# Two changes in a fused attention and two-layer MLP kernel: bf16 products of layer two left out, and another order in its last tile

## The chip, the cores and the metric

The kernel runs on one core of a Trainium2 chip. The metric is the device time of one execution, in microseconds (us). The time before is the median of three runs.

## The reference, cut to what matters

The kernel computes a two-part attention and two MLP layers behind it. The attention (4 batches, 8 heads, 576 positions, head dimension 64) adds a pooled part and a local part; its result, 2304 tokens of 512 features, goes through two layers of the same form:

```python
def mlp(x, w_in, w_out):          # x 2304 x 512, w_in 512 x 2048, w_out 2048 x 512
    h = np.maximum(x @ w_in, 0.0)
    return h * h @ w_out

x = attention(q, k, v)            # (2304, 512)
x = mlp(x, moe_w_in, moe_w_out)   # layer one
return mlp(x, moe2_w_in, moe2_w_out)   # layer two
```

Only the end of layer two and eight small products inside layer two are touched by the change.

## The kernel before, in words

**Tiles and steps.** The 2304 tokens are cut into nine tiles of 256. The list `seq` holds 18 pairs of layer and tile: entries 0 to 8 are layer one, 9 to 17 layer two, so n = 17 is the last tile of layer two. The 2048 hidden features are cut into eight pieces p of 256. A *step* is one pair (n, p): the products that make 256 hidden features of a tile (`mm_h`), ReLU and square on ScalarE (`act_h`), and the products with the second weight that add this piece to the tile's output.

**Number format.** All large products are made in three: each operand is split into a high and a low part, and high x high, high x low and low x high are summed. In `mm_h` that makes 12 products for each of the two halves of a piece, 24 per step, all from line 886.

**Layer two's output.** In layer two the second matrix product is made with seven block products in place of eight, which the code calls M1 to M7. `mm_y2` (line 944) issues them at line 952: with `first` true M5, M6, M7 and M3 (12 products of TensorE), with `first` false M1, M2 and M4 (9 products); 21 in all per step. They accumulate over the eight pieces in PSUM. `seven(n, m)` says where: M1 to M4 lie in one PSUM tile of two halves (M1 and M2 in the first, M3 and M4 in the second), `at0` for odd n and `y` for even n; M5 to M7 lie in `at1`.

**The end of a tile.** `leave` (line 1041) builds the four quarters c11, c12, c21 and c22 of the tile's output in the SBUF buffer `yst`: copies of M1 on ScalarE (line 1053, for the last tile also 1056), then seven sums on VectorE (line 1074) and the store. The last tile has a path of its own: copies of M1 to c11 and c21, the sum c11 + M2 first, then the wait for all products (`("y", n, NP - 1)`), the other six sums, a 256 KB store of the upper half of the rows behind the fourth sum (line 1069) and one of the lower half at the end (line 1077).

**What sets the order.** The program order of every engine's queue comes from the class `Order`, a planner that runs when the kernel is built. Each piece of work is a generator that yields the engine it wants and an estimated duration, or a condition (`o.at(key)`) to wait for; the planner emits what it thinks can start first. Events such as `ev["yA",]` or `ev["gl", i]` are planner events: they order the emission and are no waits on the chip. Waits on the chip are put in by the framework from what each instruction reads and writes. In `products` the generator `y` issues the second products of a step; for the last step (`i == last`) it issues M1, M2, M4 first, sets `yA`, waits for the event `gl` (the low part of the last sums S), and then issues M5, M6, M7, M3.

**The bf16 products.** `KICK` (line 49) names the steps (n, 3) for n = 10 to 17. In these, ahead of the first product of `mm_h`, line 879 issues one product of the 128 x 128 bf16 identity with itself into the first 128 columns of the PSUM tile that `mm_h` then overwrites. Its result is used by nothing. There are eight of them, one per tile from the second tile of layer two on.

Of the kernel before, what the change touches and what calls it, by code (L numbers as in the profile page):

```python
# [15 lines left out]
ALU = mybir.AluOpType  # L16
# [5 lines left out]
TN = 256  # L22
NT = B * S // TN
NP = DFF // 256
# [21 lines left out]
FT = 3  # L46
LAZY = dict(split_x=1.2)
FINE, HALF = 6, 1
KICK = {(n, 3) for n in range(10, 18)}
CL, GL, HL = 4, 4, 6  # L50
CP, CD, GP, UP = -0.848, 0.436, -1.416, -1.019
QP, VP, HP = -0.537, 0.649, -0.76
# [167 lines left out]
def attention_two_mlp_kernel(  # L220
# [11 lines left out]
    nc = tc.nc  # L232
# [6 lines left out]
    ident16 = sb.tile([128, 128], BF16, name="ident16")  # L239
# [120 lines left out]
    def seven(n, m):  # L360

        t = pair[2 - 2 * (n % 2) if m < 4 else 1]
        return t[:, m % 4 // 2, m % 2 * 256:m % 2 * 256 + 256]
# [5 lines left out]
    o = Order()  # L369
    ev = o.ev  # L370

    def dve(cols):
        return "DVE", 0.065 + cols / 957.0
# [23 lines left out]
    def dma(nbytes, run=4096):  # L397

        return "SP", nbytes / (16e3 * run) * {256: 22.5, 1024: 88.0, 2048: 142.0, 4096: 212.0}[run]
# [439 lines left out]
    seq = [(layer, t) for layer in (1, 2) for t in range(NT)]  # L839
# [32 lines left out]
    def mm_h(i, fi):  # L872
        n, p = steps[i]
        h, x = xH[n % NXL], xL[n % NXL]
        wH, wL = weight(p, 0, 0), weight(p, 0, 1)
        o = hb[i % 2][:, fi * 256:fi * 256 + 256]
        if (n, p) in KICK and fi == 0:

            nc.tensor.matmul(out=o[:, 0:128], lhsT=ident16, rhs=ident16, start=True, stop=True)
        fs = slice(fi * 128, fi * 128 + 128)  # L880
        mms = []
        for kk in range(4):
            mms += [(wH, h, kk), (wL, h, kk)]
        mms += [(wH, x, kk) for kk in range(4)]
        for i, (w, x, kk) in enumerate(mms):
            nc.tensor.matmul(  # L886
                out=o, lhsT=wt[p, 0][:, 1084:1340][:, fs] if w is wL and kk == 0 and p in ODD else w[:, kk, fs],
                rhs=x[:, kk], start=(i == 0), stop=(i == len(mms) - 1)
            )
# [51 lines left out]
                nc.vector.tensor_tensor(out=late2["SL"], in0=late2["S"], in1=late2["SH"].bitcast(F32), op=ALU.subtract)  # L941
            ev["gl", i] = tt

    def mm_y2(i, first):

        n, p = steps[i]
        some = ((5, 0, "T1"), (6, 1, "T2"), (7, 2, "T3"), (3, 3, "B22")) if first else ((1, 0, "B11"), (2, 2, "B21"), (4, 3, "T4"))
        for m, a, w in some:
            cs = slice(128 * a, 128 * a + 128)
            hi, lo = (late2["SH"][:, cs], late2["SL"][:, cs]) if first else (g_of(i, 0)[:, cs], g_of(i, 1)[:, cs])  # L950
            for x, (lhsT, low) in enumerate(((hi, 0), (hi, 1), (lo, 0))):
                nc.tensor.matmul(  # L952
                    out=seven(n, m - 1), lhsT=lhsT, rhs=quarter(p, w, low),
                    start=p == 0 and x == 0 and m not in (2, 3, 6),
                    stop=p == NP - 1 and x == 2 and m in (2, 4, 6, 7), skip_group_check=True,
                )
# [24 lines left out]
    def products():  # L981
        def y(i):
            n, p = steps[i]
            yield o.at("gh", i)
            if p == 0 and n > 1 and n < NT:
                yield o.at("left", n - 1 if n != 2 else 0)
            if seq[n][0] == 2:
                if p == 0 and n > NT:
                    yield o.at("left", n - 2)
                yield o.at("T", p)  # L990
                yield o.at("gl" if i != last else "gla", i)
                for first in (0 < p and i != last, p == 0 or i == last):
                    if p == 0 and first and n > NT:
                        yield o.at("left3", n - 1)
                    if i == last and first:
                        ev["yA",] = t
                        yield o.at("gl", i)
                    t = yield "PE", 1.37 if first else 1.03
                    mm_y2(i, first)
                    if first:  # L1000
                        ev["yS", i] = t
                ev["y", n, p] = t
                return
            yield "PE", 1.825
            mm_y(i, False)
            yield o.at("gl", i)
            ev["y", n, p] = yield "PE", 0.912
            mm_y(i, True)

        for i, (n, p) in enumerate(steps):  # L1010
            o.now.prio = n + p / NP + PO
            if p == 0 and i and n < NT:
                yield from y(i - 1)
            if i == last:
                yield o.at("gl", i - 2)
                yield "PE", 1.37
                mm_h(i, 0)
                ev["h", n, p] = yield "PE", 1.37
                mm_h(i, 1)
                yield from y(i - 2)  # L1020
                yield from y(i - 1)
                break
            if p == 0:
                yield o.at("split", n)
            if i == 0:
                o.fill = None
                yield from f_at.give_up([2])
            if (n, p) == (1, 0):
                yield from f_at.give_up([1])
            yield o.at("w", seq[n][0], p)  # L1030
            if i > 1:
                yield o.at("gl", i - 2)
            yield "PE", 1.37
            mm_h(i, 0)
            ev["h", n, p] = yield "PE", 1.37
            mm_h(i, 1)
            if (p or n >= NT) and i != last - 1:
                yield from y(i - 1)
        yield from y(last)

    def leave():
        for n, (layer, t) in enumerate(seq):
            yield o.at(*(("yA",) if n == len(seq) - 1 else ("y", n, NP - 1)))
            i = yield from f_ld.take()
            yst = ld[i].bitcast(F32)
            if layer == 1:
                for u in range(2):
                    tt = yield act(512)
                    nc.scalar.copy(yst[:, u * 512:u * 512 + 512], ybs(n)[u])
            else:  # L1050
                c11, c12, c21, c22 = (yst[:, 256 * m:256 * m + 256] for m in range(4))
                yield act(256)
                nc.scalar.copy(c11, seven(n, 0))
                if n == len(seq) - 1:
                    yield act(256)
                    nc.scalar.copy(c21, seven(n, 0))
                sums = [
                    (c21, c11, 6, ALU.add), (c12, c21, 5, ALU.add), (c21, c21, 7, ALU.add), (c22, c21, 5, ALU.add),
                    (c12, c12, 3, ALU.add), (c11, c11, 2, ALU.add), (c21, c21, 4, ALU.subtract),
                ]  # L1060
                if n == len(seq) - 1:
                    sums = [sums[k] for k in (5, 0, 1, 4, 2, 3, 6)]
                    sums[1] = (c21, c21, 6, ALU.add)
                for k, (dst, a, m, op) in enumerate(sums):
                    if n == len(seq) - 1 and k == 1:
                        yield o.at("y", n, NP - 1)
                    if n == len(seq) - 1 and k == 4:
                        yield dma(128 * 2048, 2048)
                        nc.sync.dma_start(out=out[t * TN:t * TN + 128], in_=yst[:, 0:512])
                        o.now.done, o.now.last = tt, "DVE"  # L1070
                    tt = yield dve(256)
                    if dst is c22:
                        ev["left3", n] = tt
                    nc.vector.tensor_tensor(out=dst, in0=a, in1=seven(n, m - 1), op=op)
                if n == len(seq) - 1:
                    yield dma(128 * 2048, 2048)
                    nc.sync.dma_start(out=out[t * TN + 128:(t + 1) * TN], in_=yst[:, 512:1024])
                    return
            ev["left", n] = tt
            if n == 1:  # L1080
                f_at.back(1, tt)
            tt = yield dma(128 * 4096)
            if layer == 1:
                nc.sync.dma_start(out=ys[t], in_=yst)
            else:
                nc.sync.dma_start(
                    out=out[t * TN:(t + 1) * TN].rearrange("(u p) e -> p u e", p=128),
                    in_=yst.rearrange("p (u e) -> p u e", u=2),
                )
            f_ld.put(i, tt)  # L1090
            ev["stored", n] = tt

    heads, groups, vees = [], [], []
    for b in range(B):
        t = b * S / TN - 2 + (b == 1) * H1
# [33 lines left out]
    with tc.manual_schedule():  # L1129
# [3 lines left out]
        for n, (c, off, some) in enumerate(((0, 0, (0,)), (0, 3, (1, 2)), (1, 3, (0, 1)), (1, 10, (2,)))):  # L1133
            m = xr[n % 2].rearrange("p k c -> p (k c)")[:, 64 * n:64 * n + 64]
            nc.gpsimd.memset(m, 0.0)
            first = off - 64 * c
            nc.gpsimd.affine_select(
                out=m, in_=m, pattern=[[1, 64]], base=3 - first, channel_multiplier=-1,
# [39 lines left out]
```

## Time and profile before

| | us |
|---|---|
| median of three runs | 907.33 (907.09 to 908.36) |
| the profiled execution, its own time | 912.61 |
| its span, first to last instruction | 910.8 |
| TensorE busy | 888.7 (98%) |
| VectorE busy | 488.4 (54%) |
| ScalarE busy | 520.6 (57%) |
| GpSimd busy | 61.9 (7%) |

In the profile PE is TensorE's matmul, PEld its weight load, DVE VectorE, ACT ScalarE, POOL GpSimd, SP the engine that issues the DMAs; a q behind a name means the engine's sequencer. Times count from the first instruction. Layer two begins at about 485 us. A matmul's row has its start and its length; since matmuls are pipelined, the length (0.28 us) is longer than the distance from one start to the next, so a rate is read from starts or from counts, not from lengths. In a row of the timeline several like instructions are merged: start, time that they cover, and their number behind the x.

### The profile page before, as it was taken

The page shows a single profiled execution, that of the slowest core. Times are in us where ns is not written, and L with a number is a line of the kernel's source. Part 1 is how long each engine was busy: PE and PEld are TensorE (multiplying, and loading weights), DVE is VectorE, ACT ScalarE, POOL GpSimd, SP SyncE. Part 2 cuts the span into 40 slices and gives each one's busy share as a digit, 9 for nine tenths or more (in the row PEclk, how much of TensorE's full clock was granted, in tenths as well). Part 3 has the DMA queues.
Part 4 walks back from the last instruction along what each step waited for, and adds up shares of the span by engine and source line. Part 5 has one row for each costly group of instructions (what it writes and reads, how often), then busy time and mean ns, then how long its engine had stood idle before and what let it go on. Part 6 is the DMA issues. An engine that isn't in the chain of part 4 may idle for free.

```text
span 910.8 us, 20739 instructions
## 1 busy us (share of the span) xinstructions
PE 888.7 (98%) x8701; PEld 857.3 (94%) x8701; DVE 488.4 (54%) x1035; ACT 520.6 (57%) x969; POOL 61.9 (7%) x70
## 2 busy tenths in 40 slices
PE   8888899999999999999999999999999999999997
PEld 5578899999999999999999999999999999999996
DVE  5695673475874535233323665546555464645454
ACT  3896884466467665644435674545554554545443
POOL 3310310020220100000001000000000000000000
PEclk9989899999999999999999999999999999999999
DMA  9999951353465675621214630101010000100000
GB/s 181 230 228 193 218 134 35 93 142 87 104 205 175 218 223 197 197 82 30 82 35 163 210 121 24 47 2 47 1 47 24 24 25 24 44 5 24 1 25 24
DMA packets 94013, 90.47 MB, mean 99 GB/s; under 512 B 62432, under 2 KB 70368, under 8 KB 93920
## 3 DMA queue, kind: packets, MB, share of 16 engines
q1 hardware_dynamic: 93920, 89.15, 36.2%
q8 instruction: 68, 1.11, 0.5%
q14 instruction: 25, 0.20, 0.1%
HBM read 70.25 MB, written 18.87 MB: 98 GB/s over the span
## 4 chain that ended last, share of the span: by engine, by line
PE 89%; DMA 6%; SPq 2%; DVE 1%; ACT 1%; issue 0%; ACTq 0%
PE h L886 42%; PE y L969 19%; PE at L952 14%; PE y L952 5%; DMA ld<-in_v_dram 3%; PE at L969 2%; DMA s<-in_moe_w_out_dram 2%; DMA s<-in_moe_w_in_dram 2%; PE at L455 1%; SPq L442 1%; PE at L646 1%; PE at L591 1%; PE at L481 1%; PE at L521 1%; PE at L628 1%; PE at L511 1%
## 5 line engine op out<-in xcount | busy, mean ns | idle before, releaser
L886 PE MATMUL h<-xH,w 128*128 128x256 f32 x2304 | 317.5, 280 | 2.1 <-ACT xH L395 2.1
L886 PEld LDWEIGHTS h<-xH,w 128*128 128x128 f32 x2304 | 287.4, 189 | 4.6 <-ACT xH L395 2.2
L969 PE MATMUL y<-g,w 128*128 128x256 f32 x1536 | 191.2, 279 | 0.0
L969 PEld LDWEIGHTS y<-g,w 128*128 128x128 f32 x1536 | 181.0, 188 | 2.7 <-issue 1.2
L886 PE MATMUL h<-xL,w 128*128 128x256 f32 x1152 | 180.4, 279 | 2.0 <-DVE xL L863 2.0
L886 PEld LDWEIGHTS h<-xL,w 128*128 128x128 f32 x1152 | 154.4, 189 | 2.5 <-DVE xL L863 2.5
L904 ACT ACTIVATE ld<-h 128x512 f32<-128x512 f32 x72 | 43.1, 598 | 133.1 <-PE h L886 133.1
L931 DVE TENSOR_TENSOR S<-ld 128x128 f32<-128x128 f32 x144 | 35.7, 289 | 153.2 <-ACT ld L906 153.2
L936 DVE TENSOR_TENSOR g<-h,g 128x512 fp32r<-128x512 f32 x72 | 49.6, 689 | 117.0 <-ACT g L908 116.6
L904 ACT ACTIVATE h<-h 128x512 f32<-128x512 f32 x72 | 42.0, 583 | 97.8 <-PE h L886 97.6
L914 ACT CAST SH<-S 128x512 fp32r<-128x512 f32 x72 | 44.8, 622 | 39.2 <-DVE S L931 29.8
L941 DVE TENSOR_TENSOR gSL<-S,SH 128x512 fp32r<-128x512 f32 x72 | 49.8, 692 | 10.8 <-ACT SH L914 2.2
L936 DVE TENSOR_TENSOR g<-ld,g 128x512 fp32r<-128x512 f32 x72 | 49.2, 684 | 0.1
L906 ACT ACTIVATE ld<-ld 128x512 f32<-128x512 f32 x72 | 45.5, 631 | 2.3
L908 ACT CAST g<-ld 128x512 fp32r<-128x512 f32 x72 | 44.8, 622 | 2.3
L952 PE MATMUL at<-w,SH 128*128 128x256 f32 x224 | 44.0, 278 | 0.0
L906 ACT ACTIVATE h<-h 128x512 f32<-128x512 f32 x72 | 42.2, 586 | 1.3
L908 ACT CAST g<-h 128x512 fp32r<-128x512 f32 x72 | 42.0, 584 | 1.4
L952 PE MATMUL at<-w,g 128*128 128x256 f32 x240 | 34.0, 277 | 0.0
L952 PEld LDWEIGHTS at<-w,SH 128*128 128x128 f32 x224 | 33.9, 188 | 0.0
L952 PE MATMUL at<-w,gSL 128*128 128x256 f32 x112 | 31.2, 279 | 0.1
L952 PEld LDWEIGHTS at<-w,g 128*128 128x128 f32 x240 | 30.4, 188 | 0.0
(251 smaller groups left out, 1276.7 us busy)
## 6 DMA issues: line engine op xcount, KB each, us to landing
s<-in_moe_w_in_dram SPq DMA_DIRECT2D x32, 256.0 KB
s<-in_moe_w_out_dram SPq DMA_DIRECT2D x16, 512.0 KB
ws<-ga SPq DMA_DIRECT2D x32, 256.0 KB
ld<-in_moe_w_in_dram SPq DMA_DIRECT2D x12, 512.0 KB
ld<-in_moe_w_out_dram SPq DMA_DIRECT2D x10, 512.0 KB
w<-ws SPq DMA_DIRECT2D x10, 512.0 KB
xr<-ys SPq DMA_DIRECT2D x9, 512.0 KB
vw<-in_v_dram SPq DMA_DIRECT2D x68, 64.0 KB
```

The costliest lines, as they stand in the source:

```text
L442: nc.sync.dma_start(out=raw[:, z].rearrange("p (h d) -> p h d", h=H), in_=(q, k)[z][b, :, 128 * c:128 * c + n].rearrange("h s d -> s h d"),)
L455: nc.tensor.transpose(pair[a][:, z, 128 * m:128 * m + n], raw[:, z, 128 * m:128 * m + 128], ident[0:n, 0:n])
L886: nc.tensor.matmul(out=o, lhsT=wt[p, 0][:, 1084:1340][:, fs] if w is wL and kk == 0 and p in ODD else w[:, kk, fs], rhs=x[:, kk], start=(i ...
L904: nc.scalar.activation(out=g, in_=h, func=AF.Relu)
L906: nc.scalar.activation(out=g, in_=g, func=AF.Square)
L908: nc.scalar.copy(g_of(i, 0), g)
L914: nc.scalar.copy(late2["SH"], late2["S"])
L931: nc.vector.tensor_tensor(out=dst, in0=a, in1=b, op=op)
L936: nc.vector.tensor_tensor(out=g_of(i, 1), in0=g, in1=g_of(i, 0).bitcast(F32), op=ALU.subtract)
L941: nc.vector.tensor_tensor(out=late2["SL"], in0=late2["S"], in1=late2["SH"].bitcast(F32), op=ALU.subtract)
L952: nc.tensor.matmul(out=seven(n, m - 1), lhsT=lhsT, rhs=quarter(p, w, low), start=p == 0 and x == 0 and m not in (2, 3, 6), stop=p == NP - ...
L969: nc.tensor.matmul(out=yb[e // 2][:, (e % 2) * 256:(e % 2) * 256 + 256], lhsT=w[:, fi, e * 128:e * 128 + 128], rhs=g[:, fi * 256:fi * 256 ...
```

## The change

Three edits:

1. `KICK` and the bf16 product of line 879 are left out.
2. In the last step `y` issues M1, M2, M4 as before, then M6, M7, M5 (`mm_y2` with `some`), sets `yB`, then waits for the planner's event `copied`, and then issues M3 alone. `copied` is set by `leave` behind the two copies of M1 and the sum c11 + M2, which so stand ahead of M3 in program order.
3. The last tile's copies go to c11 and c12 (not c21), the sums come in another order, and there are three stores in place of two: the upper 128 rows in full, then the left and the right half of the lower 128 rows.

```diff
-KICK = {(n, 3) for n in range(10, 18)}
...
-        if (n, p) in KICK and fi == 0:
-
-            nc.tensor.matmul(out=o[:, 0:128], lhsT=ident16, rhs=ident16, start=True, stop=True)
...
-    def mm_y2(i, first):
+    def mm_y2(i, first, some=None):
...
-        some = ((5, 0, "T1"), (6, 1, "T2"), (7, 2, "T3"), (3, 3, "B22")) if first else ((1, 0, "B11"), (2, 2, "B21"), (4, 3, "T4"))
-        for m, a, w in some:
+        all = ((5, 0, "T1"), (6, 1, "T2"), (7, 2, "T3"), (3, 3, "B22")) if first else ((1, 0, "B11"), (2, 2, "B21"), (4, 3, "T4"))
+        for m, a, w in [all[j] for j in some] if some else all:
...
                     if i == last and first:
+
                         ev["yA",] = t
                         yield o.at("gl", i)
+                        t = yield "PE", 1.03
+                        mm_y2(i, True, (1, 2, 0))
+                        ev["yB",] = t
+                        yield o.at("copied")
+                        t = yield "PE", 0.34
+                        mm_y2(i, True, (3,))
+                        break
...
                 if n == len(seq) - 1:
                     yield act(256)
-                    nc.scalar.copy(c21, seven(n, 0))
+                    nc.scalar.copy(c12, seven(n, 0))
+                    rows = out[t * TN:(t + 1) * TN].rearrange("(u p) e -> u p e", u=2)
+                    for dst, a, m, op, wait, to in (
+                        (c11, c11, 2, ALU.add, None, None), (c12, c12, 6, ALU.add, ("yB",), None),
+                        (c22, c12, 7, ALU.add, None, None), (c12, c12, 5, ALU.add, None, None),
+                        (c12, c12, 3, ALU.add, ("y", n, NP - 1), (rows[0], yst[:, 0:512])),
+                        (c21, c22, 4, ALU.subtract, None, (rows[1][:, 0:256], c21)),
+                        (c22, c22, 5, ALU.add, None, (rows[1][:, 256:512], c22)),
+                    ):
+                        if wait:
+                            yield o.at(*wait)
+                        tt = yield dve(256)
+                        nc.vector.tensor_tensor(out=dst, in0=a, in1=seven(n, m - 1), op=op)
+                        if m == 2:
+                            ev["copied",] = 0.0
+                        if to:
+                            yield dma(128 * 1024, 1024)
+                            nc.sync.dma_start(out=to[0], in_=to[1])
+                            o.now.done, o.now.last = tt, "DVE"
+                    return
...
-                if n == len(seq) - 1:
-                    sums = [sums[k] for k in (5, 0, 1, 4, 2, 3, 6)]
-                    sums[1] = (c21, c21, 6, ALU.add)
-                for k, (dst, a, m, op) in enumerate(sums):
-                    if n == len(seq) - 1 and k == 1:
-                        yield o.at("y", n, NP - 1)
-                    if n == len(seq) - 1 and k == 4:
-                        yield dma(128 * 2048, 2048)
-                        nc.sync.dma_start(out=out[t * TN:t * TN + 128], in_=yst[:, 0:512])
-                        o.now.done, o.now.last = tt, "DVE"
+                for dst, a, m, op in sums:
...
-                if n == len(seq) - 1:
-                    yield dma(128 * 2048, 2048)
-                    nc.sync.dma_start(out=out[t * TN + 128:(t + 1) * TN], in_=yst[:, 512:1024])
-                    return
```

## Rows read from the trace of the kernel before

**Rows 1.** The page: busy shares, and the chain's shares by engine.

```profile
PE 888.7 (98%) x8701; PEld 857.3 (94%) x8701; DVE 488.4 (54%) x1035; ACT 520.6 (57%) x969; POOL 61.9 (7%) x70
...
PE 89%; DMA 6%; SPq 2%; DVE 1%; ACT 1%; issue 0%; ACTq 0%
```

**Rows 2.** Windows: from:to, length, busy us (instructions) by engine, granted clock, DMA.

```profile
440.00:580.00 140.00, 140.00 (x1236) 140.00 (x1235) 68.25 (x141) 79.62 (x145) 5.17 (x7) 1.00 0.32 106
584.00:624.00 40.00, 40.00 (x342) 40.00 (x341) 20.44 (x53) 19.56 (x33) 0.00 (x0) 1.00 0.08 27
626.00:665.00 39.00, 39.00 (x346) 39.00 (x346) 20.72 (x53) 19.63 (x34) 0.00 (x0) 1.00 0.08 28
...
877.00:897.00 20.00, 20.00 (x179) 20.00 (x178) 8.81 (x23) 9.26 (x15) 0.00 (x0) 1.00 0.01 2
...
582.24:880.62 298.38, 298.38 (x2576) 298.10 (x2574) 160.85 (x406) 149.81 (x248) 0.00 (x0) 1.00 0.07 24
```

**Rows 3.** Line 879, the bf16 products: count, length, first and last start.

```profile
L879 PE MATMUL h<-ident x8: 230/230/230, 582.2 to 875.4; 128*128 128x128 bf16 x8
```

**Rows 4.** Timeline of TensorE: where steps of layer two begin.

```profile
582.24 0.23 PE L879 MATMUL h<-ident 128*128 128x128 bf16 x1
...
587.67 0.52 PE L886 MATMUL h<-xH,w 128*128 128x256 f32 x3
...
624.77 0.23 PE L879 MATMUL h<-ident 128*128 128x128 bf16 x1
...
630.02 1.07 PE L886 MATMUL h<-xH,w 128*128 128x256 f32 x8
...
665.78 0.23 PE L879 MATMUL h<-ident 128*128 128x128 bf16 x1
```

**Rows 5.** The chain that ended last, from the copies on: start, us, what.

```profile
904.83 0.76 DVE ld L1074 x2
...
905.61 0.43 DVE ld L1074
...
906.07 0.76 DVE ld L1074 x2
...
907.30 0.42 DVE ld L1074
```

**Rows 6.** Timeline of ScalarE and TensorE at the end.

```profile
904.15 0.37 ACT L1053 COPY ld<-at 128x256 f32<-128x256 f32 x1 [2.75 <-PE at L952]
904.42 0.38 ACT L1056 COPY ld<-at 128x256 f32<-128x256 f32 x1
...
902.42 0.28 PE L952 MATMUL at<-q_vw,g 128*128 128x256 f32 x1
902.53 0.40 PE L952 MATMUL at<-w,SH 128*128 128x256 f32 x2
...
903.59 0.40 PE L952 MATMUL at<-w,SH 128*128 128x256 f32 x2
903.83 0.28 PE L952 MATMUL at<-w,gSL 128*128 128x256 f32 x1
```

**Rows 7.** Timeline of TensorE: two restarts after a wait.

```profile
438.37 1.00 PEld L969 LDWEIGHTS y<-g,w 128*128 128x128 f32 x8 [0.19 <-ACT g L908]
...
899.13 0.19 PEld L952 LDWEIGHTS at<-w,gSL 128*128 128x128 f32 x1 [0.28 <-DVE gSL L941]
...
899.13 0.38 PE L952 MATMUL at<-w,gSL 128*128 128x256 f32 x1
```

**Rows 8.** SP's stores and its wait, and the DMA strip of 907 to 910.8.

```profile
907.75 0.34 SPq L1077 DMA_DIRECT2D out_dram<-ld  x1
...
SPq L1173 <- DMA out_dram<-ld: 1.6, 1, 1.6
...
DMA  0002989999920000289999992000000000000000
```

## The prediction

> **What bounds the kernel now.** I read the page's busy shares and its chain first: TensorE is busy for 98% of the span and holds 89% of the chain that ends last [rows 1]. So in layer two a time is a number of products times the distance between their starts. The windows show the clock granted in full (1.00, the 2.4 GHz level) in each of these stretches of layer two, and no other engine near its limit: VectorE and ScalarE are busy 20 of 39 to 40 us [rows 2]. But the products do not come at one rate: the stretch 440 to 580 holds 1236 in 140 us, 584 to 624 holds 342 in 40 us, 626 to 665 holds 346 in 39 us, and 877 to 897 has 179 in 20 [rows 2]. What lies between them and nowhere else is the bf16 product of line 879: there are eight, one in each tile, the first at 582.24 and the last at 875.37 [rows 3].
>
> The timeline of TensorE gives the size. A step of layer two is 24 products of line 886 and 21 of line 952, 45 in all. From 587.67, the step behind the first bf16 product, to the second at 624.77 there are 7 steps in 37.10 us: 5.300 each, 0.1178 us a product, the **wide** spacing. From 630.02 to the third at 665.78 there are 7 in 35.76 us: 5.109 each, 0.1135 us a product, the **narrow** one [rows 4]. Each bf16 product turns narrow into wide or wide into narrow, and what it set holds to the next one; this pair of tiles comes four times. The steps that begin with one take 5.43 us (582.24 to 587.67) and 5.25 us (624.77 to 630.02), so its own slot costs 0.13 to 0.14 us over the spacing that follows it [rows 4].
>
> The end is the second place where a wait counts. After the last product starts at 903.83, ScalarE's two copies, seven VectorE sums and a store follow one another: copy at 904.15, the first sum at 904.83, the last sum over at 907.72, and the store behind it [rows 5, 6].
>
> **The change part by part.** *The eight bf16 products out.* From the first one to the end of the last one's step the core spends 298.38 us (582.24 to 880.62) on 57 steps [rows 2, 4]. Without them nothing that the trace shows would turn the spacing: it is narrow when the first one comes, and it held through 140 us without one [rows 2]. Then the 57 steps take 57 x 5.109 = 291.2 us: **7.2 us less**, of which 4 x 0.13 + 4 x 0.14 = 1.1 us is the products' own slots and 32 x 0.191 = 6.1 us the steps with wide spacing. The whole is TensorE time on the chain, so no cover is needed or lost; what the other engines must do per step fits, since in the narrow stretch 626 to 665 they have half of the time free [rows 2]. The steps from 880.62 on are narrow already (179 in 20 us) and stay [rows 2]. Bounds: if wide spacing came without a cause for all 57 steps, 57 x 5.300 = 302.1, 3.7 us more than now; if none, 7.2 less. I take the latter, by the stretch ahead of the first one, 440 to 580.
>
> The Trainium skill's page "TensorE: Matmul & The Clock Gate", section "Back-to-back issue gap", gives one distance per shape, N/2.4 plus about 2.5 ns, so 109 ns for 256 columns. By it the kernel would have no second spacing to lose, and the whole edit would be worth the slots alone. The trace disagrees: one shape at one granted clock stands at 0.1135 and at 0.1178.
>
> *Copies and one sum ahead of M3.* Now the copy of M1 waits 2.75 us for TensorE, and starts at 904.15, behind the last product of M3 (903.83 and 0.28 long), though the first product behind M4 starts at 902.53 [rows 5, 6]. M1 to M4 of this tile share the PSUM tile at0; I read the wait as one on all products into that tile that stand ahead in the program. With M3 behind the copies they wait for M4's last product alone (902.42 + 0.28 = 902.70). The copies then stand at 902.73 and 903.00, and the first sum, which now follows the second copy's end by 0.03 [rows 6], at 903.41 instead of 904.83: 1.42 us earlier. ScalarE is free then: its wait of 2.75 began at 901.40.
>
> *M3 behind them.* If the tile's writers wait for its readers in the same way, M3's three products, which would be due at 903.59, wait for that sum (903.41 + 0.42) and start near 903.88 with one slower start (0.38 for the first product after a wait [rows 7]), and end near 904.5, 0.4 us later than now. Queued behind them on TensorE is nothing; only the fifth sum waits for them. M6, M7, M5 fill the gap: nine products from 902.53 on, the last one over by 903.76 (903.59 less 0.12, and 0.28 long).
>
> *The sums.* There are seven as before. Starts lie 0.34 apart where a sum doesn't need the one before it and 0.45 where it does (904.83 to 905.61 holds two, then 906.07) [rows 5]. In the new order: c11 + M2 at 903.41, c12 + M6 at 903.80, c22 at 904.25, c12 + M5 at 904.70, c12 + M3 at 905.16 (M3 was over at 904.5, so no wait), c21 at 905.50, c22 at 905.95, over at 906.37 against 907.72: 1.35 us earlier. So the later M3 is hidden by three sums; without that cover it would cost 0.4.
>
> *Three stores in place of two.* One issue on SP takes 0.34 us [rows 8]. The first is issued at 905.61, the second at 905.96, the third at 906.40, each ready when SP is. In the profile a 256 KB store begins to move 0.8 us behind its issue, moves for 0.75 us, and SP's wait for it is over 1.6 us behind the issue's end [rows 8]. The last one has 128 KB, half of the movement (-0.35 us by that rate), but it comes behind 384 KB which start at 906.4 and need 1.1 us: it moves from 907.5 to 907.9 and has landed 0.5 later, near 908.4 instead of 909.8. I take **1.4 us less** at the end. Bounds: 1.7 (sums and the half store in full) and 0.3 (the copies wait for M5's last product too, at 903.76; the sums start at 904.47, M3 waits for them, and only the half store remains). The nearest row is the copy's own wait, so I stay at 1.4.
>
> The Trainium skill's "PSUM — Partial Sum Buffer", section "PSUM bank collisions raise a hardware error", asks for guards by bank and quadrant only, and M3 lies in the other bank of that tile. By it the copies would need M2 alone, 0.36 us earlier, and the end would gain about 1.8. The trace disagrees: the copy of M1 waited 2.75 us, for M3.
>
> The sum is 7.2 + 1.4 = 8.6 us. The profiled execution took 912.61 us with a span of 910.8; the median of the three runs is 907.33, 5.28 lower. Nothing tells that the 5.28 lie in layer two, so I take 8.6 off the median: **898.7 us**.
>
> **The rivals.** *Wide spacing from the start (slower).* Which spacing holds is settled where TensorE restarts after a wait: the restart at 438.37 gave the narrow one [rows 2, 7], the one at 899.13 the wide one (902.53 to 903.59, nine products, 0.1178 each) [rows 6, 7]. If the timed runs enter layer two wide, before is 4 x (5.25 + 35.76 + 5.43) + 3 x 37.10 = 297.1 us in those 57 steps, and without the bf16 products 302.1: 5.0 slower, less 1.4 at the end: 910.9. If only the changed kernel does, 3.7 - 1.4 = 2.3: 909.6. It decides as soon as over 45 of the 57 steps (8.6 / 0.19) are wide. For it: both outcomes stand in one trace. Against: the one stretch that settled it here came out narrow, and three runs within 1.3 us can't have entered differently, since 440 to 582 alone differs by 1270 x 0.0045 = 5.7 us.
>
> *Wide for a part.* A wait in layer two that the trace of before doesn't have makes the spacing wide for the rest; for half of the 57 steps that gives back 28 x 0.19 = 5.4: 904.1. Three quarters give back 8.2: 906.9, no change that shows. For it: narrow crossings into an odd tile (11, 13, 15, 17) do not occur now. Against: the even ones do, with no idle time.
>
> *The bf16 products don't set the spacing.* Something with the tile does, and they only stand where it turns: then they are worth their slots, 1.1, with 1.4 at the end: 904.8. Against: eight turns of eight fall on them to the product. It is also what the one distance per shape in the Trainium skill's "TensorE: Matmul & The Clock Gate" comes to.
>
> **How the numbers follow.** Forecast 0.70; wide for about half 0.08; slots alone 0.04; wide for about three quarters, or runs of both kinds with a median near that of before, 0.05; wide throughout 0.13. A measurement of this kernel can tell about 0.2%, 1.8 us, from no change. Faster: 0.70 + 0.08 + 0.04 = 0.82; same 0.05; slower 0.13. The forecast's own range is 897.6 to 900.8: the bounds of the end (898.4 to 899.8) and the runs' spread of 1.3 around them. To hold eight in ten the whole range goes from there over the two middle cases (904.1 and 904.8) to 905.5; the last two cases, 0.18, stay outside.
>
> **What would show it.** Right: between 583 and 897 every window of 40 us holds about 355 products, steps of 5.10 to 5.13 us throughout, and no line of bf16 products; a copy of M1 near 902.7 less 7.2, that is 895.5, with M3 a little behind it; the last sum over 1.9 us behind the end of M3's products and no longer 3.6; three issues on SP 0.35 to 0.45 apart. Wrong: 342 in 40 us anywhere behind 440; a copy that still starts behind M3 or M5; a fifth sum that waits for TensorE; a third store that lands over 2.2 us behind its issue.

## The result

The changed kernel takes 898.33 us in the median of six runs (896.70 to 899.86), the kernel before 907.17 us in six (905.35 to 908.36). The ratio is 0.9904 with a 95% interval of 0.9888 to 0.9920: 8.8 us less. Forecast were 898.7 us and 8.6 us less.

The page of the profiled execution (its own time 898.71 us, span 896.9 us) shows the same shares as before [rows 1]: TensorE fills the span and holds the chain. First the line of busy shares, then the chain's shares by engine:

```profile
PE 881.7 (98%) x8693; PEld 849.5 (95%) x8693; DVE 489.3 (55%) x1035; ACT 520.8 (58%) x969; POOL 61.5 (7%) x70
...
PE 91%; DMA 4%; ACT 2%; SPq 1%; DVE 1%; issue 0%; POOL 0%; ACTq 0%; POOLq 0%; DVEq 0%
```

The windows of layer two tell where the time went (columns as in [rows 2]: stretch, length, busy us and instructions of PE, PEld, DVE, ACT, POOL, granted clock, DMA share, GB/s). The last one goes from the first product of tile 10, piece 3 (where the first bf16 product stood) to the first of tile 17, piece 4:

```profile
434.00:574.00 140.00, 140.00 (x1235) 140.00 (x1235) 68.25 (x141) 79.62 (x145) 5.17 (x7) 1.00 0.32 106
578.00:618.00 40.00, 40.00 (x354) 40.00 (x354) 21.87 (x57) 20.25 (x35) 0.00 (x0) 1.00 0.08 28
620.00:660.00 40.00, 40.00 (x355) 40.00 (x354) 21.74 (x56) 21.12 (x35) 0.00 (x0) 1.00 0.08 28
830.00:870.00 40.00, 40.00 (x355) 40.00 (x353) 21.41 (x55) 20.05 (x33) 0.00 (x0) 1.00 0.04 15
576.67:867.96 291.29, 291.29 (x2568) 291.29 (x2566) 160.66 (x406) 149.81 (x248) 0.00 (x0) 1.00 0.07 25
```

Every 40 us now hold 354 or 355 products; the wide stretches with 342 [rows 2] are gone, at the same granted clock of 1.00. The 57 steps take 291.29 us where they took 298.38 with the bf16 products' own slot at the front [rows 2], or 298.34 measured from the same product of line 886: 7.05 us less.

In the last tile the copies of M1 no longer wait for M3. This is the timeline: ScalarE's two copies, TensorE from the last product of M4 (889.76) to the last one of M3 (891.57), and SP's issues:

```profile
890.07 0.37 ACT L1057 COPY ld<-at 128x256 f32<-128x256 f32 x1 [1.33 <-PE at L948]
890.34 0.38 ACT L1060 COPY ld<-at 128x256 f32<-128x256 f32 x1
...
889.76 0.28 PE L948 MATMUL at<-q_vw,g 128*128 128x256 f32 x1
...
890.82 0.28 PE L948 MATMUL at<-w,gSL 128*128 128x256 f32 x1
891.23 0.51 PE L948 MATMUL at<-w,SH 128*128 128x256 f32 x2
891.57 0.28 PE L948 MATMUL at<-w,gSL 128*128 128x256 f32 x1
...
893.02 1.31 SPq L1077 DMA_DIRECT2D out_dram<-ld  x3
```

The first copy starts 0.03 us behind the end of M4's last product (889.76 + 0.28 = 890.04); before, it started behind M3's [rows 6]. M3 pays for it: due at 890.94, it starts at 891.23. The waits of that stretch put this down to line 1072, the first sum; the other row is SP's wait for the stores (who waited for whom, us in total, times, longest):

```profile
PEld at L948 <- DVE ld L1072: 0.3, 1, 0.3
...
SPq L1183 <- DMA out_dram<-ld: 1.5, 1, 1.5
```

The chain that ended last, from the first sum on (start, us, what):

```profile
890.75 0.81 DVE ld L1072 x2
...
891.59 0.43 DVE ld L1072
...
892.04 0.43 DVE ld L1072
...
892.57 0.76 DVE ld L1072 x2
...
893.35 0.42 DVE ld L1072
```

The sums follow one another without a wait for M3; seven take 3.02 us, against 2.90 before [rows 5]. Last the DMA strip of 893 to 896.9 in 40 slices:

```profile
DMA  0000000028999998999999982000000000000000
```

The three stores, issued from 893.02 to 894.33, move without a break from 893.8 to 895.4, and SP's wait for them is 1.5 us. From the first product of the last step to the end of the span it takes 16.03 us; before it took 17.27. That is 1.24 us less.

So the two parts are 7.05 and 1.24 us, 8.3 together. The two spans differ by 13.9 us; the other 5.6 lie ahead of the first place of a bf16 product, which this profile reaches at 576.67 and the one of before at 582.28. The twelve experiments below reach it between 573.8 and 580.7, whatever they change behind it. So nothing in the change explains those 5.6: the profiled execution of before was late there, and the medians, 8.84 apart, are the measure.

### The profile page after: what moved, and what is told of

Read it like the earlier page. It is cut to its first block, busy times and chain, and to the rows that moved or that the text cites. A ratio compares the mean times of both kernels' runs of the same rounds, so it can differ in the third digit from the quotient of the medians.

```text
span 896.9 us, 20726 instructions
## 1 busy us (share of the span) xinstructions
PE 881.7 (98%) x8693; PEld 849.5 (95%) x8693; DVE 489.3 (55%) x1035; ACT 520.8 (58%) x969; POOL 61.5 (7%) x70
## 4 chain that ended last, share of the span: by engine, by line
PE 91%; DMA 4%; ACT 2%; SPq 1%; DVE 1%; issue 0%; POOL 0%; ACTq 0%; POOLq 0%; DVEq 0%
PE h L882 43%; PE y L965 19%; PE at L948 14%; PE y L948 5%; PE at L965 3%; DMA s<-in_moe_w_out_dram 2%; PE at L454 1%; DMA ld<-in_v_dram 1%; PE at L645 1%; PE at L590 1%; PE at L480 1%; PE at L520 1%; PE h L1133 1%; PE at L627 1%; PE at L510 1%; DMA e<-in_v_dram 1%
```

## The experiments

All kernels start from the changed kernel unless it is said otherwise. "57 steps" and "end" are the two measures used above: from the first product of line 886 (or its place) in tile 10, piece 3, to the one in tile 17, piece 4; and from the last step's first product to the end of the span. Where a time below is that of a single run, it can't tell a microsecond or two (the six runs of the changed kernel alone differ by 3.2 us); there the rows of the profile decide.

| kernel | 57 steps, us | end, us |
|---|---|---|
| before | 298.34 | 17.27 |
| changed | 291.29 | 16.03 |
| eight products back | 298.34 | 15.89 |
| old last tile, no products | 291.29 | 17.13 |
| one product | 302.18 | 16.05 |
| eight pairs | 292.73 | 15.89 |
| one f32 product of 128 columns | 291.38 | 16.04 |
| one f32 product of 256 columns | 291.29 | 15.88 |
| one bf16 product of 256 columns | 302.18 | 16.04 |
| three products, then two | 291.56 | 15.90 |
| one, two, three, one | 296.70 | 16.05 |
| two single ones elsewhere | 295.10 | 16.04 |
| M3 ahead of the copies | 291.29 | 17.18 |
| two stores | 291.29 | 15.85 |

**The products alone, put back.** The last tile stays as changed.

```diff
+KICK = {(n, 3) for n in range(10, 18)}
...
+        if (n, p) in KICK and fi == 0:
+            nc.tensor.matmul(out=o[:, 0:128], lhsT=ident16, rhs=ident16, start=True, stop=True)
```

> The changed kernel with the eight bf16 products put back; its last tile stays as changed. If the two parts are independent and the products turn the spacing: the 57 steps from the first product to the end of the last one's step take 298.3 us again (291.3 without them), narrow and wide tiles alternate as before, and the time is that of the kernel before less the 1.2 to 1.3 us of the last tile: 905.9, ratio 0.9986. If the last tile were worth more than its rows show (3 us or more), it would be below 904; if the products were worth their slots alone, 899.5.

Measured: 905.10 us, ratio to before 0.9983 (0.9970 to 0.9995). The 57 steps are back at 298.34 and the end stays short, 15.89. The tiles alternate as before (columns of the windows as above):

```profile
580.00:614.00 34.00, 34.00 (x291) 34.00 (x290) 17.44 (x44) 15.69 (x28) 0.00 (x0) 1.00 0.05 17
620.00:655.00 35.00, 35.00 (x311) 35.00 (x310) 19.05 (x49) 17.47 (x29) 0.00 (x0) 1.00 0.09 31
```

The last tile alone is worth 0.17%, some 1.5 us (0.5 to 2.7 by the interval), and does not depend on the products.

**The products taken out, the old last tile.** The kernel before without the line of the bf16 product and without `KICK`.

> The kernel before with only the eight bf16 products taken out; the last tile as before. If they turn the spacing: 57 steps in 291.3 us, no wide stretch between layer two's start and the last stall, 7.05 us less than before: 900.1, ratio 0.9922; the last sum ends 5.0 us behind M4's last product as before. If the products were worth their slots alone: 906.1. If the new order of the last tile had brought the most: above 905.

Measured: 900.39 us, ratio 0.9926 (0.9910 to 0.9942). 57 steps in 291.29, the end in 17.13. The two parts add up: 0.17% and 0.74% make 0.91%, the whole change 0.96%, within the intervals. The value of the slots alone (906.1) is far outside.

**One product, at the first place.** As above with a shorter `KICK`:

```diff
+KICK = {(10, 3)}
```

> The changed kernel with one bf16 product, at the first place alone (tile 10, piece 3). If a product turns the spacing and what it set holds until something else turns it: all 57 steps behind it are wide, 5.300 us each, 302.2 us in place of 291.3, 10.9 us more: 909.2, slower than the kernel before. If the tile or the place sets the spacing, or the wide spacing relaxes back by itself: at most one wide tile, 1.6 us, or the slot alone, 0.13: 898.5 to 900.

Measured: 910.94 us, ratio 1.0044 (1.0028 to 1.0060). The windows of its profile, the first ahead of the product at 576.6, the others behind it:

```profile
440.00:560.00 120.00, 120.00 (x1060) 120.00 (x1059) 57.56 (x113) 68.87 (x126) 5.17 (x7) 1.00 0.33 113
...
580.00:620.00 40.00, 40.00 (x342) 40.00 (x341) 20.80 (x55) 20.34 (x35) 0.00 (x0) 1.00 0.08 27
640.00:680.00 40.00, 40.00 (x342) 40.00 (x341) 22.01 (x55) 19.27 (x32) 0.00 (x0) 1.00 0.08 27
720.00:760.00 40.00, 40.00 (x342) 40.00 (x341) 21.54 (x53) 19.36 (x33) 0.00 (x0) 1.00 0.08 28
```

One product of 0.23 us makes the next 300 us wide, up to the wait in the last step. Nothing in the tiles brings narrow spacing back, and nothing relaxes. The 57 steps take 302.18 (302.2 expected), and the three steps behind them another 0.48 more; the timed median is 1.7 us above the expected one, of which the 0.5 are a part and the rest is less than the interval's half width.

**Two in a row at each of the eight places.**

```diff
         if (n, p) in KICK and fi == 0:
             nc.tensor.matmul(out=o[:, 0:128], lhsT=ident16, rhs=ident16, start=True, stop=True)
+            nc.tensor.matmul(out=o[:, 0:128], lhsT=ident16, rhs=ident16, start=True, stop=True)
```

> The changed kernel with two bf16 products in a row at each of the eight places. If each turns the spacing, a pair leaves it as it was: all 57 steps stay narrow and only the slots are paid, some 8 x 0.2 = 1.6 us: 899.9. If any disturbance by bf16 products sets the spacing anew, by place or by chance, some of the eight tiles are wide: each costs 1.5 us more, and with four of them 906.

Measured: 901.01 us, ratio 0.9928 (0.9904 to 0.9953); 57 steps in 292.73. That is 1.44 more for the seven pairs that lie in this stretch (the first one stands ahead of it), 0.21 each. The windows 580 to 620 and 640 to 680 hold 355:

```profile
580.00:620.00 40.00, 40.00 (x355) 39.96 (x355) 21.55 (x57) 21.12 (x35) 0.00 (x0) 1.00 0.08 27
640.00:680.00 40.00, 40.00 (x355) 39.96 (x354) 21.70 (x56) 20.50 (x34) 0.00 (x0) 1.00 0.08 27
```

A pair leaves narrow spacing narrow. It looked like a count of turns, an even number undoing itself; the next runs tested that.

**What about the product does it.** Three kernels, each with `KICK = {(10, 3)}` and, in place of the bf16 product's line, the one shown; two have the kernel's usual f32 operands, one bf16 operands and the usual length.

```diff
+            nc.tensor.matmul(out=o[:, 0:128], lhsT=wH[:, 0, 0:128], rhs=h[:, 0, 0:128], start=True, stop=True)
```

> The changed kernel with one more product at the first place (tile 10, piece 3), of the kernel's usual f32 operands with 128 columns in place of a bf16 one. If it is the bf16 operands that turn the spacing: narrow throughout, 291.3 us for the 57 steps and the slot. If a single product of another length than the 256 columns around it is enough: wide from there on, 302.2 us, some 909 for the kernel.

```diff
+            nc.tensor.matmul(out=o, lhsT=wH[:, 0, 0:128], rhs=h[:, 0], start=True, stop=True)
```

> The changed kernel with one more product at the first place that is just like its neighbours: f32, 256 columns, without a bf16 operand. If the count of products were what matters (an odd one more turns it): wide from there on, 302.2 us for the 57 steps. If the odd product must differ from its neighbours: narrow, 291.4 us.

```diff
+            nc.tensor.matmul(out=o, lhsT=ident16, rhs=ident16.unsqueeze(1).to_broadcast([128, 2, 128]), start=True, stop=True)
```

> The changed kernel with one bf16 product at the first place that has 256 columns like the f32 products around it. If bf16 operands turn the spacing, whatever the length: wide from there on, 302.2 us for the 57 steps. If the shorter product's slot does it: narrow, 291.4 us.

Measured, one run each: 899.48, 902.57 and 910.47 us. The same stretch of each, in that order:

```profile
580.00:614.00 34.00, 34.00 (x302) 34.00 (x301) 18.47 (x49) 17.39 (x29) 0.00 (x0) 1.00 0.08 27
```

```profile
580.00:614.00 34.00, 34.00 (x302) 34.00 (x301) 18.52 (x47) 16.53 (x28) 0.00 (x0) 1.00 0.05 17
```

```profile
580.00:614.00 34.00, 34.00 (x291) 34.00 (x291) 17.46 (x46) 16.95 (x28) 0.00 (x0) 1.00 0.05 18
```

302 in 34 us is narrow, 291 wide. The f32 products leave narrow spacing, whatever their length (the short one is followed by about 1 us of wide spacing, which goes by itself). The bf16 one turns it with 256 columns as with 128: the operands matter, not the length. Which of their properties it is stays open: the bf16 products multiply the identity, the f32 ones the kernel's own data, and an f32 identity was not tried. The 902.57 of the second is not layer two: its 57 steps take 291.29, but it comes to them 4 us later (580.65 against 576.67) like the profile of before.

**Three in a row, then two.**

```diff
+KICK = {(10, 3): 3, (14, 3): 2}
...
+        for _ in range(KICK.get((n, p), 0) * (fi == 0)):
+            nc.tensor.matmul(out=o[:, 0:128], lhsT=ident16, rhs=ident16, start=True, stop=True)
```

> The changed kernel with three bf16 products in a row at the first place (tile 10, piece 3) and two at tile 14, piece 3. If every bf16 product turns the spacing: three make it wide, and the two leave it wide, 302.3 us for the 57 steps. If a group counts by how long it is and not by its number: narrow behind three, or narrow again behind the two, 291.5 to 297.

Measured: 899.17 us, 57 steps in 291.56. The stretch behind the three holds 302 in 34 us:

```profile
580.00:614.00 34.00, 34.00 (x302) 34.00 (x302) 18.50 (x49) 17.77 (x30) 0.00 (x0) 1.00 0.08 31
```

Three do not turn narrow spacing. So bf16 products don't each turn the spacing, and the theory of a count of turns falls.

**One, two, three and one.** As above with

```diff
+KICK = {(10, 3): 1, (12, 3): 2, (14, 3): 3, (16, 3): 1}
```

> The changed kernel with one bf16 product at tile 10, two in a row at tile 12, three at tile 14 and one at tile 16 (piece 3 each). Three in a row left narrow spacing narrow, so a count of products does not turn it. If only a single one turns the spacing and a longer group leaves it as it is: wide from tile 10 to tile 16, 48 steps, 291.3 + 48 x 0.191 = 300.5 us for the 57 steps and 0.5 for the slots. If a group of two or three always ends in narrow spacing, whatever was before: wide for the 16 steps up to tile 12 and, behind the last single one, for the 9 from tile 16 on, 296.3.

Measured: 904.44 us, 57 steps in 296.70 (296.3 expected of groups that end narrow, 300.5 of groups that leave things as they are). Its windows: two behind the one, two behind the pair, one behind the last:

```profile
580.00:614.00 34.00, 34.00 (x291) 34.00 (x290) 17.97 (x48) 16.63 (x29) 0.00 (x0) 1.00 0.07 24
620.00:655.00 35.00, 35.00 (x299) 35.00 (x298) 18.52 (x46) 16.66 (x28) 0.00 (x0) 1.00 0.05 16
670.00:695.00 25.00, 25.00 (x222) 25.00 (x221) 12.96 (x34) 12.29 (x21) 0.00 (x0) 1.00 0.00 1
705.00:740.00 35.00, 35.00 (x311) 35.00 (x310) 19.44 (x50) 18.11 (x30) 0.00 (x0) 1.00 0.09 31
...
830.00:860.00 30.00, 30.00 (x258) 30.00 (x256) 15.20 (x40) 13.68 (x23) 0.00 (x0) 1.00 0.01 1
```

Wide behind the single one (291 in 34, 299 in 35), narrow behind the pair (222 in 25, 311 in 35), wide again behind the last single one (258 in 30). A pair takes wide spacing to narrow and leaves narrow as it is; a single one takes either to the other. Three were met only by narrow spacing, here too, and leave it.

**Single products elsewhere.** One in the middle of a step, one at another piece:

```diff
+KICK = {(12, 6, 1), (15, 1, 0)}
...
+        if (n, p, fi) in KICK:
```

> The changed kernel with one bf16 product in the middle of a step (ahead of the second half of tile 12, piece 6) and one at the start of tile 15, piece 1. If a single bf16 product turns the spacing wherever it stands: wide between the two, 18.5 steps, 3.5 us, and narrow elsewhere, 294.9 us for the 57 steps. If the place at piece 3 matters: narrow throughout, 291.5.

Measured: 903.06 us, 57 steps in 295.10 (294.9 expected). Narrow up to 675.7, where the first one stands, wide behind it, narrow behind the second at 775.1:

```profile
620.00:655.00 35.00, 35.00 (x311) 35.00 (x310) 19.48 (x51) 17.75 (x30) 0.00 (x0) 1.00 0.09 30
...
705.00:740.00 35.00, 35.00 (x300) 35.00 (x299) 19.10 (x49) 17.05 (x29) 0.00 (x0) 1.00 0.08 30
...
790.00:820.00 30.00, 30.00 (x267) 30.00 (x266) 16.18 (x42) 14.48 (x25) 0.00 (x0) 1.00 0.04 14
```

At these two places a single product does what it does at piece 3.

**M3 ahead of the copies again.** The other two edits of the last tile stay.

```diff
-                        yield o.at("copied")
...
-            yield o.at(*(("yA",) if n == len(seq) - 1 else ("y", n, NP - 1)))
+            yield o.at("y", n, NP - 1)
```

> The changed kernel with M3's products back ahead of the copies of M1 in program order; the new order of the sums and the three stores stay. If a copy waits for every product into its PSUM tile that stands ahead of it: it starts behind M3, 1.4 us later, M3 waits for nothing, and from the last step's first product to the end it takes 17.3 us in place of 15.9 to 16.0. If the copies were free to start behind M2 and the gain came from the order of the sums: 15.9 to 16.0.

Measured: 898.67 us in one run; the end takes 17.18 (17.3 expected). The copy waits for M3 again:

```profile
890.14 0.37 ACT L1056 COPY ld<-at 128x256 f32<-128x256 f32 x1 [2.59 <-PE at L948]
...
889.83 0.28 PE L948 MATMUL at<-w,gSL 128*128 128x256 f32 x1
```

With the spacing narrow in its last products, as here, the kernels with copies ahead need 15.88 to 15.90. So the place of the copies, ahead of M3, is worth 1.3 us, and that is all that the last tile gains: the old last tile with narrow spacing took 17.13, this one 17.18. The runs show that the copy waits for M3, whose result it doesn't read. They don't tell a wait on all products into its PSUM tile from one on all products that stand ahead of it: M3 is both.

**Two stores.** The lower half in one store behind the last sum.

```diff
-                        (c21, c22, 4, ALU.subtract, None, (rows[1][:, 0:256], c21)),
-                        (c22, c22, 5, ALU.add, None, (rows[1][:, 256:512], c22)),
+                        (c21, c22, 4, ALU.subtract, None, None),
+                        (c22, c22, 5, ALU.add, None, (rows[1], yst[:, 512:1024])),
```

> The changed kernel with two stores in place of three: the lower half of the rows in one store of 256 KB behind the last sum. If the third store gains what its smaller size moves faster: 0.3 us longer at the end, 16.2 to 16.3 from the last step's first product to the end. If the third store gives that back in SP's queue, where it was issued 0.16 us behind its sum, not 0.03: no difference, within 0.15 of 15.9 to 16.0.

Measured: 897.69 us in one run, the end in 15.85 (15.88 to 15.90 with three stores and the same spacing). The third store brings nothing. SP's last two issues of the changed kernel, and the last one here:

```profile
893.41 0.42 SPq L1077 DMA_DIRECT2D out_dram<-ld  x1
...
893.93 0.40 SPq L1077 DMA_DIRECT2D out_dram<-ld  x1
```

```profile
892.83 0.34 SPq L1077 DMA_DIRECT2D out_dram<-ld  x1
```

With three stores the second issue still runs when the last sum ends (893.77), and the third comes 0.16 behind that sum; with two stores the last one comes 0.03 behind it (892.80 and 892.83). The strip of 892 to 895.9 of this run shows that its data stop moving at 894.4, 1.6 us behind the last sum; with three stores they stop at 895.4, 1.6 behind it too:

```profile
DMA  0000000007999998459999995000000000000000
```

## Why the prediction was right

The forecast was 8.6 us less and 898.7 us; measured were 8.8 and 898.3. By the rows the two parts are 8.3; that the timed difference lies nearer to the forecast than the rows do is luck, within its interval of some 1.5 us to either side.

*The bf16 products out, 7.2 us.* Measured 7.05 on the same stretch, and 6.7 us in the timed runs of the kernel with this part alone (907 x 0.0074). The step "nothing that the trace shows would turn the spacing" held: narrow from 434 on in every window. It was read from 440 to 580 as a stretch of layer two, but most of that is layer one: layer two's first product starts at 525.69 in the profile of before, not at about 485. From there the eleven steps to the first bf16 product take 56.6 us, 5.14 each, so they are narrow too:

```profile
525.69 0.28 PE L886 MATMUL h<-xH,w 128*128 128x256 f32 x1
...
525.69:582.24 56.55, 56.55 (x500) 56.52 (x498) 34.69 (x91) 34.29 (x66) 0.00 (x0) 1.00 0.20 67
```

The Trainium skill's "TensorE: Matmul & The Clock Gate", section "Back-to-back issue gap", gives N/2.4 + 2.5 ns as the gap of an isolated matmul and says that in a stream of weight loads and matmuls, as here, both set the distance; for that it has figures for 128 and 512 columns and none for 256. So its 109 ns is no figure for this kernel, and "worth the slots alone", 1.1 us, was the prediction's reading of it. The runs with a single bf16 product show two distances of one shape at one granted clock.

*The reading of the turns was too wide.* "Each bf16 product turns narrow into wide or wide into narrow" is true of single ones, as before had them. Taken as a rule of bf16 products it is wrong: two in a row end in narrow spacing from either, and three leave narrow as it is. The forecast didn't need it.

*The last tile, 1.4 us.* Measured 1.24. The copies came 0.03 behind M4's end as worked out, M3 waited 0.3 for the first sum and was over 1.81 behind M4's end (1.8 worked out), and the sums hid that. Mis-sized were two small terms: the sums' chain, 3.02 us and not 2.96, since the fifth sum, which has a wait for M3, starts at 892.57, 0.10 behind the one before it, though M3 was over at 891.85 (with M3 ahead of the copies it starts 0.03 behind, and the seven take 2.90); and the stores, where "the third at 906.40, each ready when SP is" failed. The issues take 0.35 to 0.42 us here, not 0.34, and the third came 0.16 behind its sum, 0.52 behind the second, where 0.35 to 0.45 had been given as the sign. The gain that the prediction left to the smaller last store is nil.

*The guard by bank.* The Trainium skill's "PSUM — Partial Sum Buffer" ("PSUM bank collisions raise a hardware error") asks for no wait between M1's copy and M3, which lies in the other half of the tile. This program waits in both directions nevertheless: the copy for M3 when M3 stands ahead, M3 for the first sum when it stands behind, 0.3 us. "The trace disagrees" was too strong: these are the waits that the framework put in, and no run leaves them out, so none shows whether the chip needs them.

*The median.* "Nothing tells that the 5.28 lie in layer two" was the right caution: they lay ahead of the stretch.

*The rivals.* Wide spacing from the start did not come: all thirteen profiles behind the one of before reach tile 10, piece 3, narrow. The kernel with one product is the case of a changed kernel wide alone: 910.94 us measured, 909.6 in the rival (its 910.9 was for timed runs that are wide before and after). The 1270 x 0.0045 = 5.7 in that rival should be 1250 x 0.0043 = 5.4 by the prediction's own spacings; nothing hangs on it. Wide for a part did not come either: narrow crossings into the odd tiles go without a wait. That the products don't set the spacing is ruled out by the single one that changes 300 us.

## What to carry to other kernels

A stretch in which one engine is busy all the time still has a rate: count its instructions in equal windows, and where the counts differ at the same clock, look at what stands on the border. An odd instruction that costs its own 0.1 us decided here the rate of the 300 us behind it; such a thing is priced by the windows, not by its row. At the end of a kernel, place a reader in program order ahead of writers that it does not need, when its wait takes them in; the writers it delays cost nothing as long as other work stands between them and their own reader.

## What the runs showed that was not expected

The f32 products of 256 columns with their weight loads have two lasting spacings at the same granted clock of 1.00: 0.1135 us and 0.1178 us, 3.8% apart. A single bf16 product among them (0.23 us long, a slot of 0.13) changes one into the other and it stays for at least 300 us; two in a row end narrow from either, three leave narrow as it is (from wide they were not tried); one f32 product of 128 or 256 columns does not change narrow spacing for longer than about 1 us.

The rows of the weight loads differ a little with the spacing. These are line 885's in the kernel with one, two, three and one, behind the single product (wide, 600 to 614) and behind the pair (narrow, 700 to 714), with the shortest, the median and the longest in ns:

```profile
L885 PEld LDWEIGHTS h<-xL,w x20: 187/190/192, 600.0 to 611.0; 128*128 128x128 f32 x20
...
L885 PEld LDWEIGHTS h<-xL,w x21: 187/188/188, 699.9 to 713.8; 128*128 128x128 f32 x21
```

In the wide stretch every third weight load takes 192 ns, in the narrow one none takes more than 188. The bf16 product has a weight load of another length, 96 ns:

```profile
L879 PEld LDWEIGHTS <-ident x8: 96/96/96, 582.2 to 875.4; 128*128 128x128 bf16 x8
```

Why there are two spacings, and why a bf16 product changes one into the other, is open. It was not tried whether its weights or its moving operand do it.

A restart after a wait of TensorE settles it too, and not always the same way. In the last tile TensorE waits 0.3 us for the low part of S; of the eleven kernels that came to it narrow, four went on wide (before, changed, the f32 product of 128 columns, the two single ones elsewhere) and seven narrow, and the end takes 0.14 us more in the wide case (16.03 against 15.89, 17.27 against 17.13). The three that came to it wide went on narrow. Layer one's last restart, in contrast, went on narrow in every profile. What decides it at a wait is open.
